# Splitting the last two tokens of one V unit into sixteen short loads, in two blocks of an attention kernel

## The chip, the cores and the metric

The kernel runs on one core of a Trainium2 chip. The metric is the device time of one execution in microseconds. A comparison is made between kernels that run on the same chip.

## The reference

```
B, H, Sq, Skv, Dh = 8, 16, 16, 2048, 256          # q, k, v in bfloat16
scale = Dh ** -0.5
scores = einsum('bhqd,bhkd->bhqk', q, k) * scale
attn = softmax(scores, axis=-1)
out = einsum('bhqk,bhkd->bhqd', attn, v)
```

There are 128 heads, each with 16 queries of 256 numbers and its own K and V of 2048 x 256. K and V together are 268 MB, and each number of them is used once for 16 queries.

## The kernel before

The heads are worked on in 16 blocks of 8. A block's K comes in two units of 4 heads each, and so does its V. A unit is 4 MB: 128 partitions, each with 64 consecutive tokens of 256 numbers, 32 KB that lie together in HBM. The on-chip buffer `SL` has four such slots, named KA, KB, VA and VB; block 0's K goes into the V slots. `load` (L96) issues one DMA that fills some tokens `t0:t0+n` of a slot on all 128 partitions, and adds 16 to a semaphore when it has landed.

All loads of K and V go through SP's queue in an order written out by hand in `on_sync`: block 0's K, block 1's K, block 0's V, block 2's K, block 1's V, and so on; V of block `w` goes out with K of block `w + 1`. Before each load SP waits until its slot is free: `c_qk` says that the score products have read a K slot, `c_pv` that the value products have read a V slot. The last blocks' loads are cut into pieces (`TAIL_A`, `TAIL`), each with its own semaphore.

What happens to a block `g`:

- VectorE transposes each K unit in place, in 32 x 32 tiles, four instructions to a unit (L154), when `s_k` (or `s_k0` for block 0) says that it has landed.
- TensorE multiplies K with the queries (`qk`, L234 and L235) into `S_ps`, and `c_qk` is raised.
- VectorE takes the negated maximum (L156), ScalarE the exponential (L206), VectorE transposes the result (L162), ScalarE spreads it into `PTz` (L219).
- TensorE multiplies it with V (`pv`, L251): one loop over blocks, in which the value products of block `g - 1` follow the score products of block `g`. Before the first unit it waits for `s_v[0]` to reach 16 times the block's number, before the second for `s_v[1]` and, from token 32 on, `s_vc`.
- ScalarE scales the result (L180) and issues its store on its own queue (L184).

GpSimd does nothing but set `PTz` to zero at the start (L137).

Of the kernel before, what the change touches and what calls it, by code (L numbers as in the profile page):

```python
# [11 lines left out]
T = 64  # L12
KA, KB, VA, VB = 0, 1, 2, 3


def bass_standalone__softmax_full_bidir__sampling_kernel(
# [11 lines left out]
    last = G - 1  # L28
# [4 lines left out]
    vu = v.rearrange("b h s d -> (b h s) d").rearrange("(u p t) d -> u p t d", p=128, t=T)  # L33
# [3 lines left out]
    with ExitStack() as es:  # L37
        ec = es.enter_context
        SL = ec(nc.sbuf_tensor("SL", [128, 4, T, D], BF16))
# [14 lines left out]
        def sem(name):  # L54
            return ec(nc.semaphore(name))
# [4 lines left out]
        s_v = [sem("s_va"), sem("s_vb")]  # L60
# [26 lines left out]
        s_vc = sem("s_vc")  # L87
        s_kl = sem("s_kl")

        def obank(g, e):  # L90
            return e + (2 if g == last else 0)

        def kslot(g, e):
            return (VA, VB)[e] if g == 0 else (KA, KB)[e]

        def load(eng, src, g, e, slot, t0, n, s):  # L96
            eng.dma_start(SL[:, slot, t0:t0 + n, :], src[2 * g + e, :, t0:t0 + n, :]).then_inc(s, 16)  # L97

        def on_sync(eng):
            eng.dma_start(QT[:], qh).then_inc(s_q, 16)  # L100
            for e in range(2):
                load(eng, ku, 0, e, kslot(0, e), 0, T, s_k0[e])
            for g in range(1, G):
                for e in range(2):
                    if g >= 2:
                        eng.wait_ge(c_qk[e], g)
                    if (g, e) != (last, 1):
                        load(eng, ku, g, e, kslot(g, e), 0, T, s_k[e])
                    else:
                        load(eng, ku, g, e, kslot(g, e), 0, 32, s_k[e])  # L110
                        load(eng, ku, g, e, kslot(g, e), 32, 32, s_kl)
                w = g - 1
                for e in range(2):
                    if w:
                        eng.wait_ge(c_pv[e], w)
                    else:
                        eng.wait_ge(c_qk[e], 1)
                    if (w, e) != (last - 1, 1):
                        load(eng, vu, w, e, (VA, VB)[e], 0, T, s_v[e])
                        if e:  # L120
                            eng.sem_inc(s_vc, 16)
                    else:
                        load(eng, vu, w, e, VB, 0, 32, s_v[e])
                        load(eng, vu, w, e, VB, 32, 32, s_vc)

            eng.wait_ge(c_qk[0], G)
            for (a, n), s in zip(TAIL_A, s_vl):
                load(eng, vu, last, 0, KA, a, n, s)
            eng.wait_ge(c_qk[1], G)
            for (a, n), s in zip(TAIL, s_tail):  # L130
                load(eng, vu, last, 1, KB, a, n, s)
            eng.wait_ge(c_ev, 2 * last + 2)
            eng.dma_start(oh[128 * last:128 * last + 128, :], O_fin[:, last % 2, :]).then_inc(s_fin, 16)
            eng.wait_ge(s_fin, 16)

        def on_gpsimd(eng):
            eng.memset(PTz[:].rearrange("p a t c -> p (a t c)").bitcast(F32), 0.0).then_inc(c_pool, 1)  # L137

        def on_vector(eng):
            eng.memset(QW[:].rearrange("p e m x -> p (e m x)").bitcast(F32), 0.0).then_inc(c_qt, 1)  # L140
            eng.wait_ge(s_q, 16)
            qf = QT[:].bitcast(F32)
            eng.transpose(qf, qf).then_inc(c_qt, 1)  # L143
            for g in range(G):
                for e in range(2):
                    for c in range(4):
                        if g == 0 and c == 0:
                            eng.wait_ge(s_k0[e], 16)
                        elif c == 0:
                            eng.wait_ge(s_k[e], 16 * g)  # L150
                        elif (g, e, c) == (last, 1, 2):
                            eng.wait_ge(s_kl, 16)
                        x = SLf[:, kslot(g, e), 16 * c:16 * c + 16, :].rearrange("p t i -> p (t i)")
                        eng.transpose(x, x).then_inc(c_kt[e][c // 2], 1)  # L154
                eng.wait_ge(c_qk[1], g + 1)
                eng.tensor_reduce(out=negm[:, g:g + 1], in_=S_ps[:].rearrange("p c n -> p (c n)"),  # L156
                                  axis=AX.X, op=ALU.max, negate=True).then_inc(c_mx, 1)
                for h in range(2):
                    eng.wait_ge(c_ex[h], g + 1)
                    if g and h == 0:  # L160
                        eng.wait_ge(c_cp, 8 * g)
                    eng.transpose(PTc[:, 32 * h:32 * h + 32, :].rearrange("p t x -> p (t x)"),  # L162
                                  P_sb[:, 1024 * h:1024 * h + 1024]).then_inc(c_pt, 1)
                eng.tensor_reduce(out=ltot[:, g:g + 1], in_=lsum[:, g, :], axis=AX.X, op=ALU.add).then_inc(c_ri, 1)  # L164
                eng.wait_ge(c_ri, 2 * g + 1)
                eng.reciprocal(rinv[:, g:g + 1], ltot[:, g:g + 1]).then_inc(c_ri, 1)  # L166

        def on_scalar(eng):
# [9 lines left out]
            def evac(g, e):  # L178
                rows = slice(64 * e, 64 * e + 64)
                eng.activation(O_fin[rows, g % 2, :], O_ps[rows, obank(g, e), 0:D],  # L180
                               ACTF.Copy, scale=rinv[rows, g:g + 1]).then_inc(c_ev, 1)
# [48 lines left out]
        def on_tensor(eng):  # L230
# [45 lines left out]
            for (a, n), s in zip(TAIL_A, s_vl):  # L276
                eng.wait_ge(s, 16)
                ins = pv(0, KA, 1, obank(last, 0), a, a + n)
            ins.then_inc(c_pl, 1)
            for (a, n), s in zip(TAIL, s_tail):  # L280
                eng.wait_ge(s, 16)
                ins = pv(1, KB, 1, obank(last, 1), a, a + n)
            ins.then_inc(c_pl, 1)

        on_sync(nc.sync)
        on_gpsimd(nc.gpsimd)
        on_vector(nc.vector)
        on_scalar(nc.scalar)
# [29 lines left out]
```

## Time and profile before

| | |
|---|---|
| median of 3 runs | 636.19 us (635.75 to 636.29) |
| the profiled execution | 636.1 us |
| its span, from the first to the last instruction | 634.8 us |
| mean granted TensorE clock | 0.917 |
| HBM read, written | 269.48 MB, 1.05 MB |

The profile is of one execution. PE is TensorE's products, PEld its weight loads, DVE VectorE, ACT ScalarE, POOL GpSimd, SP the engine that issues the loads. Rows for DMA give a queue's packets, its bytes, and the time that its packets took as a share of all 16 DMA engines in the span or in the window asked for. A line that begins with "GB/s" or "DMA" has 40 equal slices of the span or the window. In a table of windows, each engine's busy time in the window stands with its number of instructions; the last three columns are the granted clock, the share of the 16 DMA engines that was busy, and GB/s. Packets are counted where they start, so a share in a short window can pass 1.

### The profile page before, as it was taken

To read this page: it belongs to the slowest core of one execution; us is meant where nothing else is said; L and a number is where in the kernel's file an instruction comes from. 1 tells how busy PE (TensorE), PEld (TensorE's weight loads), DVE (VectorE), ACT (ScalarE), POOL (GpSimd) and SP (SyncE) were. 2 spreads that over 40 slices of the span, in tenths; PEclk is the share of its full clock that TensorE was granted. 3 is DMA by queue.
4 is the path that set the end of the run, shared out by engine and by line. 5 is a ranking of instruction groups with operands and counts; after the bars stand their busy time and mean duration, and the time that the engine had idled before them with its cause. 6 is when DMAs were issued, how large, how long until landed. Compare 5 with 4: busy or idle time off the path is not lost.

```text
span 634.8 us, 6396 instructions
## 1 busy us (share of the span) xinstructions
PE 488.3 (77%) x3072; PEld 274.9 (43%) x2560; DVE 365.2 (58%) x210; ACT 214.8 (34%) x289; POOL 7.1 (1%) x5
## 2 busy tenths in 40 slices
PE   0738989595896958869597795967959689595998
PEld 0202828154271532716336262452724527144287
DVE  2968583763738546294562945739366393663830
ACT  1042252525035250342513325142252322524170
POOL 4000000000000000000000000000000000000000
PEclk9978999798997989969799797998979989798899
DMA  8999999999999999999999999999999999999997
GB/s 376 436 441 432 428 432 432 430 430 431 432 429 434 429 432 433 429 434 429 433 430 429 432 429 433 430 430 433 434 429 436 433 433 432 432 432 425 430 425 285
DMA packets 13113, 270.64 MB, mean 426 GB/s; under 512 B 1456, under 2 KB 3760, under 8 KB 4400
## 3 DMA queue, kind: packets, MB, share of 16 engines
q1 hardware_dynamic: 10944, 269.55, 98.8%
q10 hardware_dynamic: 2160, 0.98, 0.5%
q8 instruction: 3, 0.05, 0.0%
q14 instruction: 6, 0.05, 0.0%
HBM read 269.48 MB, written 1.05 MB: 426 GB/s over the span
## 4 chain that ended last, share of the span: by engine, by line
DMA 58%; PE 23%; DVE 16%; ACT 2%; issue 0%; SPq 0%
DMA SL<-in_k_dram 58%; DVE SL L154 15%; PE S_ps L234 11%; PE S_ps L235 10%; PE O_ps L251 2%; ACT PTz L219 1%; DVE PTc L162 1%; DVE negm L156 1%; ACT P_sb L206 0%; ACT O_fin L180 0%; SPq L97 0%; SPq L100 0%; DVE rinv L166 0%; DVE ltot L164 0%
## 5 line engine op out<-in xcount | busy, mean ns | idle before, releaser
L154 DVE STREAM_TRANSPOSE SL<-SL 128x2048 f32<-128x2048 f32 x128 | 284.2, 2279 | 157.9 <-DMA SL<-in_k_dram 157.9
L234 PE MATMUL S_ps<-SL,QW 128*128 128x512 bf16 x512 | 214.0, 418 | 143.5 <-DVE SL L154 143.3
L251 PE MATMUL O_ps<-SL,PTz 128*128 128x256 bf16 x2048 | 226.3, 273 | 0.9 <-ACT PTz L219 0.7
L234 PEld LDWEIGHTS S_ps<-SL,QW 128*128 128x128 bf16 x512 | 75.1, 147 | 326.6 <-issue 171.7
L251 PEld LDWEIGHTS O_ps<-SL,PTz 128*128 128x128 bf16 x2048 | 199.8, 98 | 30.9 <-issue 4.5
L235 PE MATMUL S_ps<-SL,QW 128*128 128x512 bf16 x512 | 212.5, 415 | 0.0
L219 ACT ACTIVATE PTz<-PTc 32x1024 bf16<-32x1024 bf16 x128 | 134.9, 1054 | 11.3 <-ACT O_fin L180 5.9
L174 ACT ACTIVATE QW<-QT 32x256 bf16<-32x256 bf16 x64 | 26.8, 419 | 243.3 <-PE S_ps L235 236.2
L156 DVE TENSOR_REDUCE negm<-S_ps 128x1 f32<-128x2048 f32 x16 | 36.7, 2292 | 61.4 <-PE S_ps L235 61.4
L180 ACT ACTIVATE O_fin<-O_ps,rinv 64x256 bf16<-64x256 f32 x32 | 15.0, 468 | 137.6 <-PE O_ps L251 137.5
L162 DVE STREAM_TRANSPOSE PTc<-P_sb 128x1024 bf16<-128x1024 bf16 x32 | 37.9, 1224 | 20.3 <-ACT P_sb L206 20.3
L206 ACT ACTIVATE P_sb<-S_ps,negm 128x1024 bf16<-128x1024 f32 x32 | 35.3, 1109 | 25.5 <-DVE negm L156 25.5
L137 POOL MEMSET PTz<- 128x8192 f32 x1 | 6.9, 6924 | 0.3 <-POOLq L303 0.3
L206 ACT ACTIVATION_READ_ACCUMULATOR P_sb<-S_ps,negm 128x1 f32 x32 | 6.3, 196 | 0.0
L143 DVE STREAM_TRANSPOSE QT<-QT 128x2048 f32<-128x2048 f32 x1 | 2.3, 2312 | 3.7 <-DMA QT<-in_q_dram 3.7
L166 DVE RECIPROCAL rinv<-ltot 128x1 f32<-128x1 f32 x16 | 2.6, 164 | 0.5
L164 DVE TENSOR_REDUCE ltot<-lsum 128x1 f32<-128x2 f32 x16 | 1.8, 112 | 0.0
L174 ACT ACT_TABLE_LOAD x1 | 1.3, 1283 | 0.7 <-PEq L303 0.7
L140 DVE MEMSET QW<- 128x1024 f32 x1 | 0.9, 912 | 1.0 <-PEq L303 1.0
L303 POOL MEMSET const-bfloat16-1.0<- 128x1 bf16 x1 | 0.1, 101 | 0.0
L303 POOL MEMSET const-uint8-127<- 128x1 uint8 x1 | 0.1, 101 | 0.0
L303 POOL MEMSET const-float32-0.0<- 128x1 f32 x1 | 0.1, 98 | 0.2 <-issue 0.2
(1 smaller groups left out, 0.1 us busy)
## 6 DMA issues: line engine op xcount, KB each, us to landing
SL<-in_k_dram SPq DMA_DIRECT2D x31, 4096.0 KB, 25.8
SL<-in_v_dram SPq DMA_DIRECT2D x29, 4096.0 KB, 29.1
SL<-in_k_dram SPq DMA_DIRECT2D x2, 2048.0 KB, 23.7
SL<-in_v_dram SPq DMA_DIRECT2D x2, 2048.0 KB, 29.2
SL<-in_v_dram SPq DMA_DIRECT2D x1, 2368.0 KB, 21.6
SL<-in_v_dram SPq DMA_DIRECT2D x1, 1728.0 KB, 25.4
SL<-in_v_dram SPq DMA_DIRECT2D x1, 1216.0 KB, 20.7
QT<-in_q_dram SPq DMA_DIRECT2D x1, 1024.0 KB, 4.9
```

The costliest lines, as they stand in the source:

```text
L137: eng.memset(PTz[:].rearrange("p a t c -> p (a t c)").bitcast(F32), 0.0).then_inc(c_pool, 1)
L154: eng.transpose(x, x).then_inc(c_kt[e][c // 2], 1)
L156: eng.tensor_reduce(out=negm[:, g:g + 1], in_=S_ps[:].rearrange("p c n -> p (c n)"), axis=AX.X, op=ALU.max, negate=True).then_inc(c_mx, 1)
L162: eng.transpose(PTc[:, 32 * h:32 * h + 32, :].rearrange("p t x -> p (t x)"), P_sb[:, 1024 * h:1024 * h + 1024]).then_inc(c_pt, 1)
L166: eng.reciprocal(rinv[:, g:g + 1], ltot[:, g:g + 1]).then_inc(c_ri, 1)
L174: eng.activation(ap_of(dv, dv.offset, [[1024 + 512, 2], [2, 64], [1, 2]]), ap_of(sv, sv.offset + 2 * (8 * r + a), [[8, 2], [64, 64], [1, 2]]),
L180: eng.activation(O_fin[rows, g % 2, :], O_ps[rows, obank(g, e), 0:D], ACTF.Copy, scale=rinv[rows, g:g + 1]).then_inc(c_ev, 1)
L206: eng.activation(P_sb[:, 1024 * h:1024 * h + 1024], S_ps[:, 2 * h:2 * h + 2, :].rearrange("p c n -> p (c n)"), ACTF.Exp, bias=negm[:, g:g ...
L219: eng.activation(PTz[32 * a:32 * a + 32, z, :, 64 * e + 16 * a:64 * e + 16 * a + 16], sv[:, :, 16 * (a % 2):16 * (a % 2) + 16], ACTF.Copy) ...
L234: return eng.matmul(dst, w, x, start=start, stop=stop)
L235: return eng.add_instruction(mybir.InstMatmult(name=nc.get_next_instruction_name(), engine=PE, start_tensor_calc=start, stop_tensor_calc=stop,
L251: ins = eng.matmul(O_ps[:, bank, 0:D], PTz[:, z, t, :], SL[:, slot, t, :], start=(t == 0), stop=(t == T - 1))
```

## The change

In blocks 0 and 8 the first unit of V is no longer one load. One load brings tokens 0 to 61 of all 128 partitions. Tokens 62 and 63, 1 KB in each partition, come in 16 more loads: one of 1 partition, one of 2, and so on up to 15 (120 partitions in all), and one of the remaining 8. Each of the 17 loads has a semaphore of its own. GpSimd waits for all 17, and then adds to `s_v[0]` the 16 that the one load added before; TensorE's wait is as it was. The other loads, their order and their waits stay.

```
+        SPLIT = (0, 8)
+        ROWS = [(n * (n - 1) // 2, n) for n in range(1, 16)] + [(120, 8)]
+        s_vm = sem("s_vm")
+        s_vr = [sem("s_vr%d" % i) for i in range(len(ROWS))]
...
-                    if (w, e) != (last - 1, 1):
+                    if w in SPLIT and e == 0:
+                        load(eng, vu, w, e, VA, 0, T - 2, s_vm)
+                        for (p, n), x in zip(ROWS, s_vr):
+                            eng.dma_start(SL[p:p + n, VA, T - 2:T, :], vu[2 * w + e, p:p + n, T - 2:T, :]).then_inc(x, 16)
+                    elif (w, e) != (last - 1, 1):
                         load(eng, vu, w, e, (VA, VB)[e], 0, T, s_v[e])
...
         def on_gpsimd(eng):
             eng.memset(PTz[:].rearrange("p a t c -> p (a t c)").bitcast(F32), 0.0).then_inc(c_pool, 1)
+            for i in range(len(SPLIT)):
+                for x in [s_vm] + s_vr:
+                    eng.wait_ge(x, 16 * i + 16)
+                eng.sem_inc(s_v[0], 16)
```

## The prediction

> **What bounds the kernel now.** I read the page first (busy time, slices, queues, chain), then the chain of the end, then the DMA view in short windows.
>
> ```profile
> span 634.8 us, 6396 instructions
> PE 488.3 (77%) x3072; PEld 274.9 (43%) x2560; DVE 365.2 (58%) x210; ACT 214.8 (34%) x289; POOL 7.1 (1%) x5
> DMA  8999999999999999999999999999999999999997
> DMA packets 13113, 270.64 MB, mean 426 GB/s; under 512 B 1456, under 2 KB 3760, under 8 KB 4400
> q1 hardware_dynamic: 10944, 269.55, 98.8%
> q8 instruction: 3, 0.05, 0.0%
> q14 instruction: 6, 0.05, 0.0%
> DMA 58%; PE 23%; DVE 16%; ACT 2%; issue 0%; SPq 0%
> ...
> 557.59 24.80 DMA SL<-in_k_dram
> 582.41 17.67 DVE SL L154 x8
> 618.53 14.16 PE O_ps L251 x128
> ```
>
> No compute engine is full, and the 16 DMA engines are busy in every slice; SP's queue alone takes 98.8% of their time. The last three lines are from the chain of the end: the first unit of K's last block lands at 582.4, and from there 52.4 us of transposes, products and softmax run to the end without another wait for DMA. So whatever delays that landing delays the end by the same amount, and whatever does not reach it costs nothing. A load lands when the last of its 16 engines is done. The question is therefore what the change does to the slowest DMA engine, not to the mean.
>
> The same view in two windows of 12 us, 15 to 27 and 572 to 584, shows when packets start (40 slices of 0.3 us):
>
> ```profile
> GB/s 0 0 655 1092 0 0 655 1092 0 0 655 1092 0 0 655 1092 0 0 655 1092 0 0 655 1092 0 0 655 1092 0 0 328 1420 0 0 218 1529 0 0 218 1420
> GB/s 218 437 983 109 218 437 983 109 218 437 983 109 218 437 983 109 109 546 901 218 109 546 874 109 109 382 437 492 437 328 382 437 382 492 328 492 382 492 382 495
> ```
>
> Early, all 16 engines start their packets within two slices of four, so they run within 0.6 us of each other. Late, starts fall in every slice: the engines have drifted apart by 1.2 us or more. How far shows where the work runs out (DMA share is the last column but one), and one cause shows in the window 75.2 to 76.6:
>
> ```profile
> 629.00:630.00 1.00, 1.00 (x11) 0.89 (x10) 0.00 (x0) 0.00 (x0) 0.00 (x0) 1.00 0.56 197
> 630.00:631.00 1.00, 1.00 (x12) 0.90 (x10) 0.00 (x0) 0.00 (x0) 0.00 (x0) 1.00 0.33 119
> 631.00:632.00 1.00, 1.00 (x12) 0.90 (x10) 0.00 (x0) 0.00 (x0) 0.00 (x0) 1.00 0.04 14
> q8 instruction: 1, 0.02, 4.9%
> ```
>
> In these three us 9, then 5.3, then 0.6 of 16 engines are at work; the last load ends at about 631.8 (613.0 + 18.8, rows below). Until then the mean engine idles 0.44 + 0.67 + 0.76 = 1.9 us, and the slowest not at all. One code fetch occupies one engine for 4.9% of 16 x 1.4 us = 1.10 us; the page has three of these and six of half the size. I read the lag as theirs: a few engines have been held back, and nothing gives the time back, because the queue never runs dry.
>
> **The change, part by part.**
>
> *The loads.* In blocks 0 and 8 the 4 MB load loses 1 KB of the 32 KB in each row, and 128 rows of 1 KB come in 16 loads. Prices come from three windows: 14 to 24 (one 4 MB load exactly), 631 to 632 (the last pieces, 1 KB rows) and 634 to 634.8 (the last store, 512 B rows):
>
> ```profile
> DMA packets 144, 4.19 MB, mean 419 GB/s; under 512 B 16, under 2 KB 16, under 8 KB 16
> q1 hardware_dynamic: 144, 4.19, 97.1%
> DMA packets 17, 0.01 MB, mean 14 GB/s; under 512 B 3, under 2 KB 17, under 8 KB 17
> q1 hardware_dynamic: 17, 0.01, 4.2%
> DMA packets 144, 0.07 MB, mean 82 GB/s; under 512 B 16, under 2 KB 144, under 8 KB 144
> q1 hardware_dynamic: 144, 0.07, 28.3%
> ```
>
> The 4 MB load takes 97.1% of 160 = 155.4 us of engine time in 128 rows and 16 small packets, which close the load on each engine: 1.21 us a row, so 37 ns for each KB. The second window is 0.67 us in 14 rows and 3 closing packets, the third 3.62 us in 128 and 16. With 18.9 ns between a row of 512 B and one of 1 KB, both hold for 27 ns, 46 ns and 9 ns for the closing packet. So an engine saves 8 x 37 = 296 ns in the big load, and pays 46 + 9 = 55 ns for each short row it takes. The mean engine has 8: +0.14 us a block, +0.29 us for both.
>
> How the short rows fall on the engines, the trace doesn't show: every load in it has 128 rows. (1456 small packets over 76 loads from SP and 15 stores are 16 each, so each is spread over all 16.) The least uneven is 8 rows each, the most uneven all 128 on one engine: 128 x 46 + 16 x 9 - 296 = 5.7 us a block, 11.5 us in all. A load of n rows can occupy at most n engines. I take n engines, always beginning with the same one, since 128 rows also go one share to each engine: the first then gets 16 rows, 16 x 55 - 296 = +0.58 us a block, +1.17 us in all; the last gets none, -0.59 us in all. The Trainium skill (DMA: Bandwidth & Descriptors, section on why a DMA increments its semaphore by 16) says just that: the largest number up to 16 that divides the rows, on the lowest-numbered engines. No run here shows it.
>
> *What reaches the end.* The last engine sets the landing at 582.4. If the 16-row engine is an average one, 1.9 us ahead, its +1.17 us is hidden; if it is the last, all of it counts. If the last engine is the one with no short rows, the gain is at most 0.59 us, as far as no other engine takes its place. What made engines late (code fetches) has nothing to do with row numbers, so I give the last engine the mean, 8 rows: **+0.3 us**.
>
> *Issue on SP.* Sixteen more DMA instructions stand after V's first unit in each of the two blocks, ahead of the second unit and the next K.
>
> ```profile
> 1.17 2.09 SPq L97 DMA_DIRECT2D SL<-in_k_dram  x4
> 29.07 0.33 SPq L97 DMA_DIRECT2D SL<-in_v_dram  x1
> 37.78 0.33 SPq L97 DMA_DIRECT2D SL<-in_v_dram  x1
> 338.49 0.33 SPq L97 DMA_DIRECT2D SL<-in_v_dram  x1
> 345.48 0.33 SPq L97 DMA_DIRECT2D SL<-in_v_dram  x1
> SL<-in_v_dram SPq DMA_DIRECT2D x1, 4096.0 KB, 29.0
> ```
>
> At 0.33 to 0.52 us each they take 5.3 to 8.4 us: done by 37.8 in block 0, when the second unit's wait ends anyway, and by 347.2 in block 8, 1.7 us after it. That is cost at nothing, because the load just issued at 338.49 lands 29.0 us later (last row), at 367.5: the engines have work until then. The cover is gone only if the 16 issues took some 27 us. Thirty-two instructions more on SP may bring one more small code fetch, about 0.3 us on one engine; half of the 1.10 us above would be 0.55 us. It is in the range, not in the sum.
>
> *The gathering.* GpSimd takes 34 waits and 2 increments, with nothing queued behind them: its last work ends at 7.7. TensorE alone waits for that count.
>
> ```profile
> 0.73 6.92 POOL L137 MEMSET PTz<- 128x8192 f32 x1 [0.29 <-POOLq L303]
> 65.14 1.03 PE L251 MATMUL O_ps<-SL,PTz 128*128 128x256 bf16 x8
> 370.32 0.92 PE L251 MATMUL O_ps<-SL,PTz 128*128 128x256 bf16 x7
> ```
>
> In block 8 V's first unit lands at 367.5, its short rows by 368.4 (16 x 55 ns behind), and the products start at 370.3: 1.9 us for the relay. In block 0, where the load comes in 26.3 us or so at 55.3, there are 9 us. A step between engines costs 0.02 to 0.05 us as "issue" in the chain of the end, so 17 already satisfied waits come to 0.9 us at most. Cost nothing; if the cover were gone, TensorE would idle here off the chain, and only the next load into that slot would start later, under a queue 20 us deep.
>
> *Sum.* The profiled execution took 636.1 us for its span of 634.8, the median of the three runs is 636.19. 636.19 + 0.3 = **636.5 us**. A difference under 0.2%, 1.27 us, is about what a measurement of this kernel cannot tell from no change.
>
> **The rivals.**
>
> 1. *The last engine has the most short rows.* Condition: the code fetches fall on low engines. +1.17 us: 637.4. Still within 0.2%. Against: 15 engines of 16 have fewer.
>
> 2. *The last engine has the fewest.* -0.59 us: 635.6. The share of 0.04 after 631 says that one engine is last alone, so there is something to level; but the saving is capped by the 16 KB that it no longer moves.
>
> 3. *Slower: the closing packets stall their engine.* Each short row is followed by a closing packet on its engine, and if that holds the next row until the first has landed, the busiest engine pays far more than 55 ns. The nearest rows of short transfers:
>
> ```profile
> SL<-in_v_dram SPq DMA_DIRECT2D x1, 128.0 KB, 18.8
> out_dram<-O_fin SPq DMA_DIRECT2D x1, 64.0 KB, 1.5
> DMA packets 259, 0.33 MB, mean 110 GB/s; under 512 B 38, under 2 KB 195, under 8 KB 259
> ```
>
> Fully serial, at the 1.5 us of the last store, 16 loads take 24 us a block and 48 us in all. The third row (629 to 632) speaks against that: 38 closing packets pass in under 3 us. But there 8 rows stand between two of them, here one. With a row at 0.2 us the busiest engine loses 2 x (16 x 0.2 - 0.3) = 5.8 us, less a lead of 1.9: 640.1. It decides from 0.12 us a row, where 2 x (16 x 0.12 - 0.3) - 1.9 = 1.3. The Trainium skill (the same page, rules for kernel authors) also speaks against the change: it wants small transfers joined, since under 64 KB one pays mostly overhead, by its fit 2.0 us each. By that 16 loads in series would be 32 us a block.
>
> 4. *Slower: SP's queue is full.* It blocked at the end:
>
> ```profile
> 606.17 10.76 SPq L97 DMA_DIRECT2D SL<-in_v_dram  x3
> 613.00 3.94 SPq L97 DMA_DIRECT2D SL<-in_v_dram  x1
> ```
>
> There some ten loads were outstanding, 9 packets an engine each, about 90. If the limit is ten loads, half the short ones wait until the big one lands; the engines then run dry for 8 issues at 0.43 (between the two issue times above) and the 1.5 us of one short transfer, 5 us a block: 646. If it is packets, block 8 has 9 + 9 + 9 + 32 = 59 on the fullest engine, and nothing blocks.
>
> **How the numbers follow.** The forecast (636.5, between 636.2 and 637.0) 0.44; rival 1 0.14; rival 2 0.15; rival 3 0.14; rival 4 0.04; the rest 0.09, for causes not seen here, 0.05 of it faster. All of the forecast, and nearly all of rivals 1 and 2, are within 0.2%: same 0.71, slower 0.21 (rivals 3 and 4, and rival 1 with one more fetch), faster 0.08, for which the cap of 0.59 us leaves little. The range runs from 635.5, just below rival 2, to 638.5, which leaves out most of rivals 3 and 4.
>
> **What would show it.** Right: 32 more loads at SP, the chain of the end unchanged with K's landing near 582.7, in the window 629 to 632 a similar drain, no wait of L251 for the relay, rows of 1 KB at 46 ns. Wrong: a DMA slice that falls in slice 3 or 22 of 40 (blocks 0 and 8), landings over 1.3 us later from block 0 or 8 on (rival 3 or 4), issues of several us at 29 or 338 (rival 4), or a landing over 1.3 us earlier, which nothing here can explain.

## The result, and the profile after

The changed kernel takes 639.4 us (median of 3 runs, 639.29 to 639.4) against 636.19 us: a ratio of 1.0052, 95% interval 1.0038 to 1.0066. It is 3.2 us slower. The profiled execution took 639.4 us for a span of 638.1.

From the page after, and from its chain of the end (start, length, what):

```profile
span 638.1 us, 6446 instructions
DMA  9999999999999999999999999999999999999996
q1 hardware_dynamic: 11456, 269.56, 98.6%
q14 instruction: 6, 0.05, 0.0%
...
561.33 24.31 DMA SL<-in_k_dram
585.67 17.67 DVE SL L167 x8
621.79 14.20 PE O_ps L264 x128
```

The kernel is bound as before. From the landing of K's last block to the end it is 52.4 us again; the landing has moved from 582.4 to 585.6. Where it moved is read from the chain over the whole span, in which each K load stands with its start and length; the sum is its landing. First the kernel before, then the changed one, seven of the loads, the same in both:

```profile
56.96 17.80 DMA SL<-in_k_dram
87.51 26.38 DMA SL<-in_k_dram
127.81 25.09 DMA SL<-in_k_dram
322.60 25.29 DMA SL<-in_k_dram
362.54 24.35 DMA SL<-in_k_dram
439.11 25.77 DMA SL<-in_k_dram
479.08 25.31 DMA SL<-in_k_dram
```

```profile
57.45 18.02 DMA SL<-in_k_dram
88.21 26.25 DMA SL<-in_k_dram
128.51 25.43 DMA SL<-in_k_dram
323.56 25.39 DMA SL<-in_k_dram
363.50 26.98 DMA SL<-in_k_dram
443.04 25.42 DMA SL<-in_k_dram
482.99 24.65 DMA SL<-in_k_dram
```

The landings are later by 0.71 (75.47 against 74.76; 0.17 of it is there from the first load on), 0.57, 1.04, then still 1.06 at 348.95, then 3.59 at 390.48, 3.58, and from the last row on 3.25. So block 0 costs 0.5 us at once and 0.5 more by 153.9. Of the 2.5 us that come between 348.95 and 390.48, the landing records put 0.6 ahead of block 8's split load: the last K load before it lands at 359.40 against 357.77, 1.63 later, and a code fetch of 0.31 us lies at 352.1. The split itself adds 1.9 us; 0.3 us come back near 500.

The windows in which the work runs out (DMA share is the last column but one):

```profile
631.00:632.00 1.00, 1.00 (x12) 0.90 (x10) 0.00 (x0) 0.00 (x0) 0.00 (x0) 1.00 0.50 192
632.00:633.00 1.00, 1.00 (x12) 0.90 (x10) 0.00 (x0) 0.00 (x0) 0.00 (x0) 1.00 0.32 121
633.00:634.00 1.00, 1.00 (x11) 0.90 (x10) 0.00 (x0) 0.00 (x0) 0.00 (x0) 1.00 0.18 66
634.00:635.00 1.00, 1.00 (x11) 0.83 (x10) 0.00 (x0) 0.00 (x0) 0.00 (x0) 1.00 0.10 37
```

Before, the engines ran out within some 3 us; now it takes 5, and for the last two the mean of them is 3 and 1.6 engines. They are further apart than before.

SP's queue in block 8, and TensorE's one wait for the relay:

```profile
339.53 0.33 SPq L102 DMA_DIRECT2D SL<-in_v_dram  x1
339.90 5.92 SPq L126 DMA_DIRECT2D SL<-in_v_dram  x16
346.52 0.35 SPq L102 DMA_DIRECT2D SL<-in_v_dram  x1
PEld O_ps L264 <- POOLq L150: 0.6, 1, 0.6
```

The 16 issues take 5.92 us, the second unit follows 0.7 us after them, and the relay holds TensorE for 0.6 us.

### The profile page after: what moved, and what is told of

It is laid out like the page before. It is cut to its first block, busy times and chain, and to the rows that moved or that the text cites. A ratio compares the mean times of both kernels' runs of the same rounds, so it can differ in the third digit from the quotient of the medians.

```text
span 638.1 us, 6446 instructions
## 1 busy us (share of the span) xinstructions
PE 492.4 (77%) x3072; PEld 274.4 (43%) x2560; DVE 365.2 (57%) x210; ACT 214.8 (34%) x289; POOL 7.1 (1%) x5
## 4 chain that ended last, share of the span: by engine, by line
DMA 58%; PE 23%; DVE 16%; ACT 2%; issue 0%; SPq 0%
DMA SL<-in_k_dram 58%; DVE SL L167 15%; PE S_ps L247 11%; PE S_ps L248 10%; PE O_ps L264 2%; ACT PTz L232 1%; DVE PTc L175 1%; DVE negm L169 1%; ACT P_sb L219 0%; ACT O_fin L193 0%; SPq L102 0%; SPq L105 0%; DVE rinv L179 0%; DVE ltot L177 0%
## 5 line engine op out<-in xcount | busy, mean ns | idle before, releaser
L247 PE MATMUL S_ps<-SL,QW 128*128 128x512 bf16 x512 | 216.3, 422 | 141.3 <-DVE SL L167 141.2
L248 PE MATMUL S_ps<-SL,QW 128*128 128x512 bf16 x512 | 214.9, 420 | 0.0
```

What stands on the lines that cost most here:

```text
L247: return eng.matmul(dst, w, x, start=start, stop=stop)
L248: return eng.add_instruction(mybir.InstMatmult(name=nc.get_next_instruction_name(), engine=PE, start_tensor_calc=start, stop_tensor_calc=stop,
```

## The experiments

All figures in "us later" are medians against runs of the kernel before on the same chip. The trace has a landing record of every DMA engine for every load. "Loss per block" is worked out from these records: how much later than in the kernel before the loads behind a split block land, as the mean over all 16 engines.

**Loads or relay.** One load of 128 rows in place of the 16:

```
-  ROWS = [(n * (n - 1) // 2, n) for n in range(1, 16)] + [(120, 8)]
+  ROWS = [(0, 128)]
```

> The two tokens of the split unit come in one load of 128 rows instead of 16 loads, in blocks 0 and 8; GpSimd still relays. Stall theory (a closing packet holds back its engine by some 0.13 us when only one short row stands before it): 8 short rows and one closing packet on each engine, 8 x 46 + 9 - 296 = 0.08 us and at most 0.13 us of stall a block, so +0.2 to +0.4 us over the kernel before, within 0.2%. Rival A (short rows as such are slow, about 0.15 us each): 8 x 0.15 - 0.3 = +0.9 us a block, +1.8 us. Rival B (relay, GpSimd or SP issue): the relay is still there, so all of the +3.2 us that does not come from issuing.

636.18 against 636.01 us, ratio 1.0002 (0.9993 to 1.0011). Loss per block 0.08 us, what 8 x 46 + 9 - 296 gives. Short rows as such, the relay and GpSimd cost nothing that the times can tell; the loss is in the 16 loads. And their semaphores?

```
-  s_vr = [sem("s_vr%d" % i) for i in range(len(ROWS))]
+  s_vr = [sem("s_vr")] * len(ROWS)
-  for x in [s_vm] + s_vr: eng.wait_ge(x, 16 * i + 16)
+  eng.wait_ge(s_vm, 16 * i + 16); eng.wait_ge(s_vr[0], 256 * i + 256)
```

> The 16 uneven loads of the changed kernel, but all on one semaphore (GpSimd waits for 256), 2 waits a block instead of 17. If the stall belongs to the closing packet itself (both theories above): +3.2 us as before. If it comes from each load having a semaphore of its own, or from the row of waits at GpSimd: clearly less, at the least +0.3 us.

639.09 against 636.01 us, 1.0046 (1.0033 to 1.0060): the whole loss, with one semaphore and two waits.

**Uneven, or each load?**

```
+  ROWS = [(16 * i, 16) for i in range(8)]
```

> The two tokens come in 8 loads of 16 rows, in blocks 0 and 8: one row and one closing packet a load on every engine, nothing uneven. Stall theory: 8 x 0.18 - 0.3 = +1.15 us a block on every engine, less what overlaps at both ends (about 0.2), so +1.8 to +2.3 us whichever engine is last. Rival C (the loss is only the uneven spread of rows, a row costing 55 ns): 8 x 55 - 296 = +0.15 us a block, +0.3 us in all.

637.79 against 636.01 us, 1.0027 (1.0017 to 1.0038): 1.8 us later, loss per block 0.84 us. Nothing is uneven here, so unevenness alone is not the cause.

**One block alone**, `SPLIT = (0,)` and `SPLIT = (8,)`:

> Only block 0 is split, as in the changed kernel. Stall theory with the last engine: in block 0 the engine that was last (1.6 us behind) is not one of those with many rows, so most of the 2.6 us on the fullest engine is hidden: +0.4 to +1.0 us. Rival D (each split costs the same): +1.6 us.

637.60 against 636.01 us, 1.0024 (1.0015 to 1.0033).

> Only block 8 is split. Stall theory: the fullest engines pay 16 x 0.18 - 0.3 = 2.6 us but have not been put behind by block 0, so part is hidden under the lag of the engine that is last in the kernel before: +1.0 to +2.0 us, and the two single splits together less than the +3.2 us of both. Rival D (each split costs the same): +1.6 us, and the sum equals both.

637.64 against 636.01 us, 1.0024 (1.0014 to 1.0034). Each alone costs 1.6 us, as rival D had it, and I had expected less for block 0. The chains, against the rows of the kernel before above, show that equal ends come by different ways. Block 0 alone, then block 8 alone:

```profile
88.17 26.26 DMA SL<-in_k_dram
128.06 26.05 DMA SL<-in_k_dram
363.16 25.45 DMA SL<-in_k_dram
558.41 25.64 DMA SL<-in_k_dram
```

```profile
322.87 24.89 DMA SL<-in_k_dram
361.17 27.52 DMA SL<-in_k_dram
558.69 25.16 DMA SL<-in_k_dram
```

Block 0 alone is later by 0.5 at 114.4, by 1.2 at 154.1, by 1.7 at 388.6 and at the end (584.05 against 582.39). The loss grows at the times of code fetches; as I read it, they fall on engines that the short loads have put behind. Block 8 alone is level at 347.8, later by 1.8 at once (388.7), and by 1.5 at the end: the fetch near 493 puts the last engine of the kernel before further back, and not the one that is last here. The parts add up: in the changed kernel 1.6 us stand ahead of block 8's split, which adds 1.9, and 0.3 come back.

The landing records of block 8 alone tell the engines apart, because a load of n rows lands on n of them:

```
engine (by the loads it takes part in)      0     1     3    12    13   (the other 11)
short rows                                 16    15    13     3     2
behind the first engine, 62-token load   0.45  1.93  1.40  1.93  1.91   0.00 to 0.39 us
from there to its last short row         2.97  2.72  2.45  0.57  0.34 us
for one row                              0.19  0.18  0.19  0.19  0.17 us
```

An engine completes a one-row load every 0.18 us, not every 55 ns. It is not held for all of that time: here and in both blocks of the changed kernel, the last engine lands the 4 MB load behind 8.9 us after its last short row, where two such loads land 9.7 us apart in the kernel before. So the engine was 0.8 us into the next load when its last short row was recorded as landed.

In block 8 of the changed kernel the last engine is number 1, 3.3 us behind the first (the next is 2.75 behind), with 15 short rows. From its landing of the 62-token load to that of the load behind it is 11.56 us, against 9.71 in the kernel before: 1.85 us for 15 rows, 0.12 us each, which is 15 x 0.18 - 0.8. Less the 0.3 us saved, and with a 62-token load that itself landed 0.4 us late for its size, this is the 1.9 us of the split. Engine 0 pays 2.1 us for its 16 rows in block 0.

**One engine by itself.** 16 loads of one row, the other 112 rows in one load:

```
+  ROWS = [(i, 1) for i in range(16)] + [(16, 112)]
```

> The 16 first rows (1 KB) come in 16 loads of one row, which by the read-out all go to the first engine; the other 112 rows come in one load, 7 to each engine. Only that engine has many closing packets. Spacing theory: it pays 16 x 0.17 + 7 x 0.046 - 0.3 = 2.7 us a block and the others nothing; it starts 0.3 us behind the first and the last of the kernel before is 2.4 us behind, so the end comes 0.3 + 2 x 2.7 - 2.4 = +3.3 us later. Crowding theory: alone it is not in anyone's way, its rows pass in 55 ns each, 16 x 0.055 + 7 x 0.046 - 0.3 = 0.9 us a block, all hidden under the lag of other engines: 0 to +0.2 us.

638.92 against 636.04 us, 1.0045 (1.0029 to 1.0062): 2.9 us later, near the 3.3 of the spacing theory; crowding, as I had put it, would have cost nothing. The end is not a clean price, though: the loss per block is 0.61 and 0.85 us in the mean of all engines, 15 of which have no rows but those of the load of 112, and neither theory had that. The pace is read from the one engine itself. The window 54.0 to 54.9 of this run (slices of 22.5 ns), in which that engine alone has short rows:

```profile
DMA  5000000005000000050000000500000001010900
GB/s 46 0 0 0 0 0 0 0 0 46 0 0 0 0 0 0 0 46 0 0 0 0 0 0 0 46 0 0 0 0 0 0 0 46 0 46 0 1457 0 0
DMA packets 8, 0.04 MB, mean 43 GB/s; under 512 B 1, under 2 KB 7, under 8 KB 7
q1 hardware_dynamic: 8, 0.04, 19.3%
```

Five rows of 1 KB start 8 to 9 slices apart, 0.18 to 0.20 us, and next to nothing else starts in the window. The 46 is a rate, 1 KB in a slice; the 5 in the first line is half of 16 engines for 22.5 ns, so the first four of these rows are recorded with some 0.18 us each and not with 46 ns. In the changed kernel the wait is recorded elsewhere: a block's 128 short rows take 6.6 and 6.4 us in all, 0.05 us each, but of the long rows that start from 48 to 62 us, 27 take over 1.3 us, the longest 2.23; in the kernel before none takes over 1.23 there. In the landing records all 16 loads are 0.17 to 0.24 us apart, and the first four, which write partitions 0 to 3, 0.17 to 0.18 us.

**What else is in it: engines with no short row lose too.** In the changed kernel the mean loss per block is 0.87 and 0.97 us, where 0.14 was worked out, and even the first engine to finish is 0.3 us later. Three runs vary the rows for each closing packet and the size of the row: `ROWS = [(32 * i, 32) for i in range(4)]`; the 8 loads of 16 rows with `T - 8` for `T - 2`; and, in block 8 alone, `ROWS = [(0, 108), (108, 20)]`, which was to relieve the late engines 12 and 13 and beat the kernel before.

> The two tokens come in 4 loads of 32 rows (2 rows and one closing packet a load on every engine), in blocks 0 and 8. Against 8 loads of 16 rows (+1.8 us) and one load of 128 rows (+0.2 us). Spacing theory (closing packets of one engine can't follow each other within some 0.14 us net, and the rows between them pass in that time): 4 x 0.14 - 0.3 = +0.27 us a block, +0.5 us in all. Fixed-stall theory (each closing adds the same time, (0.84 - 0.14) / 8 = 0.087 us): 8 x 46 + 4 x (9 + 87) - 296 = +0.46 us a block, +0.9 us in all.

637.35 against 636.01 us, 1.0020 (1.0011 to 1.0029): more than either theory.

> As the 8 loads of 16 rows, but of 8 tokens: rows of 4 KB, by the line of 37 ns a KB about 157 ns and 9 for the closing packet; the first load brings 56 tokens. Spacing theory: the row now takes as long as the spacing, 8 x 0.166 - 8 x 0.148 = +0.15 us a block and up to 0.35 us if the closings come 0.19 us apart: +0.3 to +0.7 us in all. Fixed-stall theory: 8 x (0.166 + 0.087) - 1.18 = +0.84 us a block, +1.7 us in all, as with 1 KB rows.

640.95 against 636.01 us, 1.0077 (1.0063 to 1.0091): 4.9 us later, far more than either. In block 0 of its trace 28 of the 128 short rows take up to 0.17 us, as the line of 159 ns has it, and 89 take 0.30 us or more.

> In block 8 alone the two tokens come in a load of 108 rows and one of 20, which by the read-out of the runs so far go to engines 0 to 11 and 0 to 9: engines 12 to 15 get none. In block 8 engines 1, 12 and 13 are all about 1.9 us behind the first, and a later code fetch puts 12 or 13 last by 0.5 us. If the end follows the last engine, 12 and 13 gain 0.3 us, engine 1 loses 11 x 46 + 18 - 296 = 0.23 us, both meet, and the end comes 0.2 to 0.3 us earlier, under what the times can tell but seen in the landings. If lags do not add up like this: +0.1 to +0.3 us.

636.73 against 636.01 us, 1.0010 (1.0001 to 1.0019): later, not earlier, with at most 2 closing packets an engine and a loss of 0.56 us, also on engines that were given no short row (the first to finish lost 0.44). So few closing packets can hardly be the cause here.

**Crowding, first try.** Loads of 16 rows at every eighth partition: `SL[p // 16:128:8, ...]`, and the same for HBM's rows, or for one side only.

> 8 loads of 16 rows of 1 KB in blocks 0 and 8, as in the run of 8 loads, but each load takes every eighth partition (i, i + 8, ...) instead of 16 neighbours; HBM rows and partitions both so, and the output is unchanged. Spacing theory (closing packets of one engine can't come closer than some 0.14 us net): +0.84 us a block, +1.7 us in all as with neighbours. Crowding theory (16 engines that write 16 neighbouring partitions, or read 16 neighbouring rows of HBM, get in each other's way): clearly less, +0.15 to +0.4 us a block, +0.3 to +0.8 us in all.

637.60 against 636.14 us, 1.0023 (1.0014 to 1.0032): 1.5 us later instead of 1.8, a loss per block of 0.59 and 0.68 us.

> The same with rows of 4 KB, where neighbours cost +4.9 us and a row was seen to take 330 to 460 ns instead of 159. Crowding theory: rows fall to 159 to 300 ns, the cost to +0.3 to +2.5 us. Without crowding as the cause (something that grows with the bytes of a short load, such as its reads from HBM being started late): +4.9 us as before.

641.27 us, 1.0083 (1.0068 to 1.0098).

> Rows of 4 KB: neighbouring rows of HBM are written to every eighth partition (this puts eight tokens of two units of V into other partitions, so the output is not the reference's). Crowding on the SBUF side: as cheap as the run with both sides spread. Crowding on the HBM side: +4.9 us as with neighbours.

641.47 us, 1.0084 (1.0068 to 1.0099).

> Rows of 4 KB: every eighth row of HBM is written to neighbouring partitions (eight tokens of two units of V come into other partitions, so the output is not the reference's). Crowding on the SBUF side: +4.9 us as with neighbours. Crowding on the HBM side: as cheap as the run with both sides spread.

641.11 us, 1.0078 (1.0062 to 1.0093). No difference with 4 KB rows: as I had put it, crowding was refuted. But the step of 8 was badly chosen. The Trainium skill (SBUF — State Buffer, Door 1: the DMA port swizzle) says that four neighbouring partitions share one of 16 ports, and partition 32 further on the same one. By that formula, 16 neighbours lie on 4 ports, and a load at every eighth partition, with the next load's beside it, on 8 ports: the first three loads after it go to the same 8. All 16 are in use if a load takes every fourth partition over the whole width.

**Crowding, second try.** The same 4 loads of 32 rows, once neighbours, once `SL[p // 32:128:4, ...]` with HBM's rows moved alike; and one load of 128 rows of 4 KB.

> 4 loads of 32 neighbouring rows of 4 KB in blocks 0 and 8: 2 rows and one closing packet a load on each engine. Spacing theory: 2 rows take 0.32 us, longer than any spacing seen, so little is left: 4 x (2 x 159 + 9) - 8 x 148 = +0.12 us a block, +0.3 to +0.8 us in all. Crowding theory (32 neighbouring partitions are reached by half of the ways in, so 512 KB go at half rate): +1.2 us a block, +2 to +3 us in all.

641.78 against 636.04 us, 1.0085 (1.0068 to 1.0102).

> The same 4 loads of 32 rows of 4 KB, but each takes every fourth partition over the whole width. Spacing theory: as with neighbours, whatever that is. Crowding theory: all ways in are in use, +0.1 to +0.4 us a block, +0.3 to +0.8 us in all, clearly less than with neighbours.

636.24 us, 1.0002 (0.9993 to 1.0012).

> One load of 128 rows of 4 KB in blocks 0 and 8, 8 rows and one closing packet on each engine. Both theories: 8 x 159 + 9 - 1184 = +0.1 us a block, +0.2 us in all. If 4 KB rows at the same place of every 32 KB are slow to read from HBM: +1 us a block or more.

636.21 us, 1.0002 (0.9992 to 1.0011). The windows 54 to 58, neighbours and then every fourth:

```profile
DMA packets 86, 1.58 MB, mean 395 GB/s; under 512 B 22, under 2 KB 22, under 8 KB 40
q1 hardware_dynamic: 86, 1.58, 111.6%
```

```profile
DMA packets 59, 1.60 MB, mean 400 GB/s; under 512 B 4, under 2 KB 4, under 8 KB 11
q1 hardware_dynamic: 59, 1.60, 93.0%
```

With neighbours 18 rows of 4 KB (40 - 22) start in this window, with every fourth partition 7: the short rows are done sooner. In the packet records of block 0 a 4 KB row takes 0.16 us with every fourth partition, none above 0.17, and 0.29 us at the median with neighbours. As many loads, rows and closing packets: 5.7 us against 0.2 us, by which partitions, and with them which rows of HBM, a load takes. That the Trainium skill's port map is the reason fits both tries, but the runs do not show the ports, and no run moved one side alone to every fourth partition, so it is not shown which side decides. Nor were the 16 uneven loads tried over spread partitions: how much of their loss is crowding is not measured.

**The two theories' remains.**

> 4 loads of 32 rows of 1 KB in blocks 0 and 8, each on every fourth partition; with neighbours they cost +1.3 us. If that was crowding: 8 x 46 + 4 x 9 - 296 = +0.1 us a block, +0.2 us in all. If it was the closing packets (4 an engine, 0.16 to 0.18 us apart): 4 x 0.17 - 0.3 = +0.4 us a block, +0.8 to +1.3 us in all.

636.25 against 636.06 us, 1.0003 (0.9993 to 1.0012): the 1.3 us of the 4 loads of 32 neighbours were crowding, and 4 closing packets an engine are free. Their landings are 0.18 us apart on each engine even here, yet the next load lands 10.07 us after the 62-token load, as it does behind one short load. This fits the 0.8 us: four landings at this pace hold no engine up, 8 and 16 do. With 8 at the 0.195 us seen at every eighth partition it makes an estimated 8 x 0.195 - 0.8 - 0.3 = 0.5 us a block, near the 0.59 and 0.68 measured there, so that most of those was not crowding.

> As the run with 16 loads of one row, with rows of 4 KB (159 ns and 9 for the closing packet). Read from the landings of the one-row loads, which were 0.18 us apart with 1 KB: a least distance gives 0.18 us again, and the first engine pays 16 x 0.18 + 7 x 0.159 - 1.18 = 2.8 us a block, about +3 us at the end; a fixed time added to each row (0.13 us) gives 0.29 us apart, 16 x 0.29 + 7 x 0.159 - 1.18 = 4.6 us a block, +7 us at the end.

645.40 against 636.06 us, 1.0148 (1.0132 to 1.0165): 9.3 us later. The one-row loads land 0.25 to 0.29 us apart in block 0 (0.32 and 0.39 once each), also in partitions 0 to 3, and 0.21 to 0.45 in block 8: between the two readings or above, nearer to a fixed time for each. The 112 neighbouring rows of 4 KB beside it crowd the others as well, so the run does not settle what the time is made of.

No version was found that beats the kernel before.

## Why the prediction was wrong, and where it was right

- **The price of a short row** is the step that failed. I took the durations of single packets, 46 + 9 ns, as the pace of rows each with its own closing packet. An engine lands one every 0.18 us, and is itself held for 2.1 us by 16 rows, where the sum had 0.88: 0.12 to 0.14 us a row. Rival 3 was this mechanism, with the point from which it decides at 0.12 us a row, and 640.1 us at 0.2 us a row. That its sum with the 0.18 us of the landings gives the measured 639.4 is in part luck: of that pace 0.8 us a block hold nothing up, and it has neither the late 62-token loads nor the change of the last engine. I gave it 0.14, because 38 closing packets passed in under 3 us at the end of the kernel before. On 16 engines those are 2 or 3 each, with eight rows between two of them, as the text itself said; that row could not speak for one.
- **An engine without short rows saves 0.59 us**: wrong. In block 0 the first engine to finish is 0.3 us later, and the mean 0.87 us against 0.14. The loads slow engines that have no part in them, by crowding, as the runs with other rows suggest; the run that took rows away from the late engines made the kernel slower.
- **The last engine takes the mean of 8 rows**: the wrong question. At the true price the engines with many rows become the last. In block 0 the last engine was another (number 12, 3 short rows, 2 us behind), which hid most: 0.5 us. By block 8 engine 1 was the last and had 15 rows, so that all of it counted: 1.9 us. Rival 1 named that case, at the wrong price.
- **Which engine takes which row**: right. The landings follow the Trainium skill's rule (DMA: Bandwidth & Descriptors, why a DMA increments its semaphore by 16): n rows on n engines, always from the same first one.
- **Issue, code fetch, queue**: right. 5.92 us for the 16 issues in block 8, hidden; six small code fetches as before, of which one, by its time, is SP's and comes earlier; no blocked issue in the two blocks. Rival 4 did not occur.
- **The relay**: TensorE waits for it in block 8, because the last short rows landed at 371.8 instead of 368.4. It is off the chain, as the text had it for that case.
- **The end follows K's last landing**: right, 52.4 us both times.
- The Trainium skill's rule to join small transfers had the sign right. Its 2 us for each, a fit that the page gives for DMAs issued from GpSimd, in series is not what happened: 16 of them cost the fullest engine 2.1 us, and 4 cost 0.2 us or 1.3 by the partitions they cover.

## What to carry to other kernels

The recorded duration of a short packet is not the price of a load that has one packet on an engine: the wait can stand in the long packets behind. Read the pace from landings, and the price from when the load behind lands; where a price has only been seen with eight rows to a load, bound it for one row from the next nearest thing, however far. In a kernel that is bound by DMA, split a load over tokens, with all 128 partitions in each piece, or into few pieces whose partitions are spread over the whole width (4 pieces at every fourth partition cost 0.2 us here, 8 at every eighth 1.5); pieces of neighbouring partitions cost some 0.7 us a block or more in every run here. Engines that fall behind stay behind while the queue is full, so a delay shows only on the engine that is last, and a delay hidden now can come out later.

## What the runs showed of the hardware that I had not expected

- One engine completes loads of one 1 KB row some 0.18 us apart, alone or beside others, and loads of one 4 KB row mostly 0.25 to 0.29 us apart in block 0, up to 0.45 in block 8.
- Such landings come late: the engine was 0.8 us into the next load when the last of 15 or 16 landed, and four of them, 0.18 us apart, cost nothing.
- 512 KB in 4 loads of 32 neighbouring partitions in two blocks cost 5.7 us, at every fourth partition 0.2 us.
- Code fetches of 1.1 and 0.3 us on single engines, 9 in the span, go with lags that stay: at 582.4 in the kernel before, 5 of 16 engines are 1.3 to 2.4 us behind the first, each having fallen back after a fetch. It is up to 2.4 us of slack that only the last engine does not have.
